# First transposes in another order, a longer run of dummy matmuls, and input forms ahead of other VectorE work, in a one-core attention and feed-forward kernel

## The chip, the cores and the metric

The kernel runs on one core of one Trainium2 chip. The metric is the device time of one execution in microseconds. In each pairing only executions on the same chip in the same rounds are compared. The span of a profile (first to last instruction) is about 1.8 us shorter than the device time of the same execution (723.8 against 725.55 us for the kernel before).

## The reference

Two branches on the same input `x` of 2048 rows by 1024 columns, in bfloat16, mixed by a gate:

```python
def reference(A_x, A_wqkv, A_wo, B_x, B_w_gate, B_w_up, B_w_down, gate_w):
    x = A_x
    g = _sigmoid((x * gate_w).sum(-1, keepdims=True))
    a = _A_ref(x, A_wqkv, A_wo)          # 32 heads of 32, 8 keys per query, 2 rows apart; then @ wo
    b = _B_ref(x, B_w_gate, B_w_up, B_w_down)   # (gelu(x@gate) * (x@up)) @ down, inner width 3584
    return g * a + (1 - g) * b
```

## The kernel before

The 2048 rows are four chunks of 512, worked on in two halves ("sup" 0 and 1, chunks 0-1 and 2-3). Most matrix products use seven block products in place of eight. For this VectorE computes sums and differences of blocks, called *forms*: of the weights, of the inputs (`x_forms`, in-place form T3 among them) and of the down projection.

A small scheduler orders everything. Each stream yields operations; at each step the operation with the smallest estimated start plus the stream's bias is emitted. The result is one fixed order per engine. An operation whose data have not come holds up those behind it: in the profile after, VectorE stands still for 0.9 us at one load with other work next in its order.

The head of the program: row loads, five dummy matmuls while they fly, and the load of the gate vector `gcol`, 1024 elements of 2 bytes.

```python
    for j in range(NST):
        (nc.sync if j % 2 == 0 else nc.scalar).dma_start(out=xrow(j, 0, KT), in_=x[j * P:(j + 1) * P, :])
    warm = hrow[:, XR + NST, 0:SC]
    nc.vector.memset(warm, 0.0)
    for i in range(5):
        nc.tensor.matmul(banks[7][:], lhsT=warm[:, 0:P], rhs=warm, start=True, stop=True)
    # ... (cut: exp table, identity, qsum)
    with nc.allow_non_contiguous_dma(reason="gate vector, one element per partition"):
        nc.gpsimd.dma_start(out=gcol[:], in_=gate_w.rearrange("(k p) -> p k", p=P))
```

The first work of TensorE: eight groups of four transposes, each group evicted by VectorE (even groups) or ScalarE (odd groups), then the q projection of chunk 0, whose first matmuls need the first half of the contraction of all four row tiles.

```python
    def main():
        ne = 0
        for j in range(NST):
            for k0 in range(0, KT, KH):
                # ... four transposes of tile j, half k0; eviction by VectorE if ne is even, else by ScalarE
        yield from qkv_outer(0)      # contraction slice by slice, as the weight slices land
        # ... (cut)
```

The input forms of a half, the last block of the weight preparation, and the transposing DMA of the attention, which shares SyncE's queue with the weight loads:

```python
    def x_forms():
        t = tt(KH * SC)
        for sup in range(NSUP):
            # ... t1, t2; then T3 in place, which waits for the gate matmul of the even chunk; then T4
            yield dve(t, lambda b12=b12, b22=b22: V(out=b12, in0=b22, in1=b12, op=ALU.subtract), [("z", c0)], key=("xf", sup, 3))

    def load_prep(i0):               # rows of w_down and of wo, for VectorE's down-projection weight forms
        # ...
                for k in range(n):
                    nc.sync.dma_start(out=st[:, 2 * h + k], in_=v[:, k])

        o = turn(n, taking("z", lambda: nc.sync.dma_start_transpose(out=rows("z"), in_=xbuf[:, accs[h], :])), [("qk", h)],
                 pre=xb_pre(), key=("acct", h))

    w.run([(0.0, main()), (0.0, loads()), (0.0, late_x()), (0.88, wforms()), (0.0, down_forms()), (0.1, x_forms()), (1.43, qkv_forms()),
           (1.3, preps()), (0.13, attention()), (0.36, scores())])
```

## Time and profile before

| | |
|---|---|
| device time | 725.25 us, median of 3 (725.22 to 725.55) |
| span of the profile | 723.8 us |
| TensorE busy | 713.6 us |
| first real matmul / start of the last one | 7.02 us / 719.70 us |
| 512-column matmuls after the head, from the order | 3280, at 0.216 us start to start: 708.5 us |

The head of the page of the kernel before, with busy time and its share of the span:

```profile
span 723.8 us, 9915 instructions
PE 713.6 (99%) x3314; PEld 351.1 (49%) x3381; DVE 598.5 (83%) x898; ACT 315.3 (44%) x535; POOL 71.8 (10%) x128
```

TensorE bounds the kernel; nothing but its waits, its head and its tail can be won without removing matmuls. The view of waits of the kernel before, TensorE only (who waited, for whom: us in total, times, longest):

```profile
PE ps L298 <- DVE hT L296: 1.2, 1, 1.2
PE ps L1252 <- DMA hT<-in_A_x_dram: 0.5, 1, 0.5
PE ps L628 <- DVE lend L481: 0.5, 1, 0.5
PE ps L995 <- ACT m L1049: 0.4, 1, 0.4
PE ps L496 <- DVE lend L1259: 0.3, 1, 0.3
```

The first, second and fifth lines are the head; the third is T3 at 321 us, the fourth the feed-forward stage at 176 us. "Idle" is counted from the modelled end of a matmul (0.379 us after its start at full speed), about 0.16 us after the next could have started (0.216 us start to start where nothing waits), so each real loss is a little larger. The head in the timeline (start, duration, engine, line):

```profile
0.86 0.27 DVE L296 MEMSET hT<- 128x256 uint32 x1 [0.86 <-PEq L1311]
1.19 2.32 PE L298 MATMUL ps<-hT 128*128 128x512 bf16 x5 [1.19 <-DVE hT L296]
1.34 1.04 POOL L310 DMA_DIRECT2D gcol<-in_gate_w_dram  x1 [0.33 <-issue]
...
4.04 2.69 PE L1252 MATMUL ps<-hT 128*128 128x128 bf16 x32 [0.53 <-DMA hT<-in_A_x_dram]
...
5.54 1.43 DVE L1259 COPY lend<-ps 128x512 bf16<-128x512 bf16 x3 [0.43 <-PE ps L1252]
5.87 1.56 ACT L1257 COPY lend<-ps 128x512 bf16<-128x512 bf16 x3 [0.18 <-PE ps L1252]
...
7.02 0.59 PE L496 MATMUL ps<-lend,hT 128*128 128x512 bf16 x2 [0.29 <-DVE lend L1259]
```

The transposes do not run at one speed. The windows view of their line shows how many are in flight or begun in each half microsecond (the count in brackets):

```profile
4.10:4.60 0.50, 0.50 (x6) 0.50 (x7) 1.00 1.03 397
4.60:5.10 0.50, 0.50 (x8) 0.50 (x6) 1.00 1.07 402
5.10:5.60 0.50, 0.50 (x7) 0.50 (x6) 1.00 1.73 350
5.70:6.20 0.50, 0.50 (x13) 0.50 (x11) 1.00 1.13 10
```

Single starts are 0.107 us apart up to 5.61 us and 0.056 us after: the clock steps up there. (Columns: window; its length; TensorE busy and count; weight loads busy and count; granted clock; DMA share; GB/s. The clock column is no help here: the trace's record of the granted clock begins at 5.61 us, at 1.00.)

The wait at 321 us in the chain of waits, before (start, us, what):

```profile
318.72 1.34 DVE ring L576 x4
320.06 1.15 DVE lend L481
321.21 0.05 issue
321.25 0.87 PE ps L628 x3
```

VectorE, without a pause, reaches T3 (L481) late, and TensorE (L628) starts as soon as it is done.

### The profile page before, as it was taken

The page shows a single profiled execution, that of the slowest core. Times are in us where ns is not written, and L with a number is a line of the kernel's source. Part 1 is how long each engine was busy: PE and PEld are TensorE (multiplying, and loading weights), DVE is VectorE, ACT ScalarE, POOL GpSimd, SP SyncE. Part 2 cuts the span into 40 slices and gives each one's busy share as a digit, 9 for nine tenths or more (in the row PEclk, how much of TensorE's full clock was granted, in tenths as well). Part 3 has the DMA queues.
Part 4 walks back from the last instruction along what each step waited for, and adds up shares of the span by engine and source line. Part 5 has one row for each costly group of instructions (what it writes and reads, how often), then busy time and mean ns, then how long its engine had stood idle before and what let it go on. Part 6 is the DMA issues. An engine that isn't in the chain of part 4 may idle for free.

```text
span 723.8 us, 9915 instructions
## 1 busy us (share of the span) xinstructions
PE 713.6 (99%) x3314; PEld 351.1 (49%) x3381; DVE 598.5 (83%) x898; ACT 315.3 (44%) x535; POOL 71.8 (10%) x128
## 2 busy tenths in 40 slices
PE   8999999999999999999999999999999999999997
PEld 5666644444444444455665444444444444444443
DVE  1799999999999899799599976999999995794200
ACT  2353465557655532035552114567558557110110
POOL 1000433343121100100000000000000000001000
PEclk9999999999999999999999999999999999999999
DMA  9944799989989979945239999786566657999992
GB/s 313 236 149 103 222 354 318 334 256 349 267 218 193 274 239 299 344 143 146 58 97 300 362 324 309 236 186 177 157 178 159 177 157 178 313 326 331 327 304 99
DMA packets 180931, 172.12 MB, mean 238 GB/s; under 512 B 56464, under 2 KB 137360, under 8 KB 180880
## 3 DMA queue, kind: packets, MB, share of 16 engines
q1 hardware_dynamic: 172048, 143.69, 68.5%
q0 software_dynamic: 8544, 27.27, 10.7%
q8 instruction: 26, 0.43, 0.2%
q10 hardware_dynamic: 288, 0.52, 0.2%
q14 instruction: 25, 0.20, 0.1%
HBM read 129.50 MB, written 28.31 MB: 218 GB/s over the span
## 4 chain that ended last, share of the span: by engine, by line
PE 83%; DVE 8%; DMA 4%; issue 4%; POOL 1%; ACT 0%; DVEq 0%; POOLq 0%; ACTq 0%
PE ps L995 35%; PE ps L1159 28%; PE ps L628 12%; PE ps L496 8%; DMA fforms<-ring 1%; DVE ring L457 1%; DVE ring L576 1%; DVE hT L1058 1%; DMA ring<-in_B_w_down_dram 1%; DMA ring<-in_A_wqkv_dram 1%; DMA hT<-in_A_wo_dram 1%; DMA hT<-in_B_w_down_dram 1%; DVE hT L1120 1%; DVE hT L1039 1%; DVE hT L433 0%
## 5 line engine op out<-in xcount | busy, mean ns | idle before, releaser
L995 PEld LDWEIGHTS <-ring 128*128 128x128 bf16 x1568 | 153.2, 98 | 185.8 <-issue 1.6
L995 PE MATMUL ps<-lend,ring 128*128 128x512 bf16 x877 | 210.5, 379 | 1.3 <-ACT m L1049 0.4
L995 PE MATMUL ps<-tf,ring 128*128 128x512 bf16 x659 | 162.6, 379 | 0.7
L1159 PE MATMUL ps<-ring,hT 128*128 128x512 bf16 x696 | 159.7, 379 | 0.6
L1159 PEld LDWEIGHTS <-hT 128*128 128x128 bf16 x708 | 69.2, 98 | 83.3
L945 DVE TENSOR_TENSOR xbuf<-xbuf,lend 128x2048 bf16<-128x2048 bf16 x64 | 77.4, 1215 | 7.5 <-DMA xbuf<-xbuf 7.5
L798 DVE TENSOR_TENSOR xbuf<-qo,lend 128x2048 bf16<-128x2048 bf16 x64 | 76.7, 1216 | 0.1
L804 DVE TENSOR_TENSOR xbuf<-xbuf 128x2048 bf16<-128x2048 bf16 x56 | 68.2, 1217 | 0.3
L628 PEld LDWEIGHTS <-ring 128*128 128x128 bf16 x384 | 49.3, 129 | 34.4 <-DVE lend L481 0.9
L1024 ACT COPY ps<-ps 128x512 f32<-128x512 f32 x56 | 32.0, 571 | 55.6 <-PE ps L995 55.5
L1067 ACT ACTIVATE gl<-ps 128x512 bf16<-128x512 f32 x56 | 33.5, 598 | 49.6 <-PE ps L995 48.5
L1194 ACT ACTIVATE ost<-ps,omg 128x512 bf16<-128x512 f32 x16 | 11.0, 688 | 100.6 <-PE ps L1159 81.9
L1186 POOL DMA_DIRECT2D out_dram<-ost x24 | 13.0, 540 | 411.0 <-ACT ost L1194 319.1
L1159 PE MATMUL ps<-ring,qo 128*128 128x512 bf16 x187 | 48.5, 379 | 0.2
L466 POOL DMA_DIRECT2D fforms<-ring x56 | 30.6, 546 | 175.3 <-DVE ring L457 166.1
L628 PE MATMUL ps<-lend,ring 128*128 128x512 bf16 x203 | 47.0, 380 | 0.7 <-DVE lend L481 0.5
L1039 DVE TENSOR_TENSOR hT<-hT,gl 128x1024 bf16<-128x1024 bf16 x56 | 38.3, 683 | 11.3 <-ACT hT L1036 11.3
L953 DVE TENSOR_TENSOR xbuf<-xbuf 128x1024 bf16<-128x1024 bf16 x64 | 42.0, 683 | 0.4
L1079 DVE TENSOR_TENSOR u<-ps,u 128x512 f32<-128x512 f32 x56 | 38.3, 684 | 4.6 <-PE ps L995 3.2
L628 PE MATMUL ps<-tf,ring 128*128 128x512 bf16 x173 | 40.1, 379 | 0.2
L1058 DVE TENSOR_TENSOR hT<-ps,m 128x512 bf16<-128x512 f32 x56 | 38.2, 683 | 1.5 <-PE ps L995 1.4
L1075 ACT COPY u<-ps 128x512 f32<-128x512 f32 x56 | 32.9, 587 | 15.1 <-PE ps L995 15.1
(110 smaller groups left out, 697.1 us busy)
## 6 DMA issues: line engine op xcount, KB each, us to landing
ring<-dforms SPq DMA_DIRECT2D x112, 256.0 KB, 5.3
ring<-in_B_w_down_dram SPq DMA_DIRECT2D x84, 256.0 KB, 4.6
ring<-in_B_w_gate_dram SPq DMA_DIRECT2D x56, 256.0 KB, 4.8
fforms<-ring POOLq DMA_DIRECT2D x56, 256.0 KB, 5.3
ring<-fforms SPq DMA_DIRECT2D x56, 256.0 KB, 4.0
ring<-in_B_w_up_dram SPq DMA_DIRECT2D x42, 256.0 KB, 4.7
ring<-in_A_wqkv_dram SPq DMA_DIRECT2D x32, 256.0 KB, 5.4
ring<-oforms SPq DMA_DIRECT2D x32, 256.0 KB, 5.7
```

The source lines that it names most:

```text
L496: nc.tensor.matmul(banks[bk][:], lhsT=lhsT, rhs=xT(c, kt), start=(kt == 0), stop=(kt == KT - 1))
L628: nc.tensor.matmul(banks[bk][:], lhsT=lhsT, rhs=rhs[:, kt, :], start=(start and kt == 0), stop=(kt == KH - 1), skip_group_check=True)
L798: V(out=w3(box[t]), in0=q_b, in1=k_w, op=ALU.mult)
L804: V(out=w3(box[0]), in0=w3(box[0]), in1=w3(box[t]), op=ALU.add)
L945: return dve(tt(n), taking(("p", t), lambda: V(out=w3(box["p", t]), in0=w3(box["ab"]), in1=v_w, op=ALU.mult)), [("qkv", c, 2, t), abo] + ( ...
L953: V(out=s4(t)[:, t % 2], in0=w3(box["p", t])[:, 0:4], in1=w3(box["p", t])[:, 4:8], op=ALU.add)
L995: nc.tensor.matmul(banks[bk][:], lhsT=wv[:, k, fl * P:(fl + 1) * P], rhs=rhs[:, k, :], start=(start and k == 0), stop=(k == KH - 1), skip_ ...
L1039: yield dve(tt(2 * SC), lambda f=f: nc.vector.tensor_tensor(out=hrow[:, f, :], in0=hrow[:, f, :], in1=gl[f][:], op=ALU.mult), [e, ev[f, "g ...
L1058: ev[f, "up2"] = dve(tt(SC, True), lambda f=f: nc.vector.tensor_tensor(out=hs(f, 1), in0=v3(banks[Bk[f]][:]), in1=v3(m5[f][:]), op=ALU.add ...
L1067: nc.scalar.activation(out=gl[f][:, SC:2 * SC], in_=banks[A[f]][:], func=ACT.Gelu_apprx_tanh)
L1079: e = dve(tt(SC, True), lambda f=f: nc.vector.tensor_tensor(out=u2[f][:], in0=banks[Dk[f]][:], in1=u2[f][:], op=ALU.add), [o, ev[f, "u2"]])
L1159: nc.tensor.matmul(banks[bk][:], lhsT=l, rhs=wv[:, i, :], start=(start and k == 0), stop=(q == last and i == 1), skip_group_check=True)
```

## The change

Its intent: have the first contraction half of all rows ready one group sooner; keep TensorE busy until the rows land so that its clock is up earlier than the 5.61 us of before; and let the input forms of a half go ahead of other VectorE work, so that TensorE does not wait for T3.

```diff
-    warm = hrow[:, XR + NST, 0:SC]
+    warm = xbuf[:, 0, 0:2]
     nc.vector.memset(warm, 0.0)
-    for i in range(5):
-        nc.tensor.matmul(banks[7][:], lhsT=warm[:, 0:P], rhs=warm, start=True, stop=True)
+    for n_ in [SC] * 6 + [P] * 3:
+        nc.tensor.matmul(banks[7][:, 0:n_], lhsT=warm[:, 0:1].to_broadcast([P, P]), rhs=warm[:, 1:2].to_broadcast([P, n_]),
+                         start=True, stop=True)
 ...
-        for j in range(NST):
-            for k0 in range(0, KT, KH):
+        for j, k0 in ((0, 0), (0, KH), (1, 0), (1, KH), (2, 0), (3, 0), (2, KH), (3, KH)):
+            if True:
 ...
-(0.1, x_forms())
+(-1.0, x_forms())
```

The bias acts on both halves: the input forms of chunks 0 and 1 move too. The order of TensorE's real work does not change.

More of the change, by code (lines that the diff above doesn't have):

```diff
@@ L1292, in main @@
                 yield from q_move(c0 + 3)
-    w.run([(0.0, main()), (0.0, loads()), (0.0, late_x()), (0.88, wforms()), (0.0, down_forms()), (0.1, x_forms()), (1.43, qkv_forms()),
+    w.run([(0.0, main()), (0.0, loads()), (0.0, late_x()), (0.88, wforms()), (0.0, down_forms()), (-1.0, x_forms()), (1.43, qkv_forms()),
            (1.3, preps()), (0.13, attention()), (0.36, scores())])
```

## The prediction

> **What bounds the kernel.** TensorE. The page's first part has PE busy 713.6 of 723.8 us, clock 0.999. By the program's order 3280 matmuls of 512 columns follow the dummies and first transposes; at the trace's 0.216 us start to start that is 708.5 of the 712.9 us between the first real matmul (7.02 us) and the end of the last (719.9). Gate matmuls explain about 2.5 us more. Left to win are the head and a few PE waits, in the view of waits and the single starts: 0.50 us at 321.25 (on T3, VectorE's in-place input form of the second half), 0.3 to 0.4 us at 176.15 (ScalarE's m copy, behind a 99% busy VectorE), about 0.15 us at 93.4. The 3.9 us tail is untouched.
>
> **What the change does.**
> 1. Dummies: 5 of 512 columns (427 ns apart from 1.19 us) become 6 of 512 and 3 of 128, after a smaller memset (0.27 us today). At the trace's cold pitches (427, 107 ns) they last 2.9 us, to about 3.9, so the 0.53 us gap before the transposes nearly closes. [...] the transposes' pitch drops from 107 to 56 ns at 5.61 us. [...]
> 2. Transposes: the first half of all rows is done after six groups, not seven, but PE still does all eight first. Today the first matmul waits 0.29 us for VectorE's fourth eviction (6.54 to 6.97); in the new order the last one needed is ScalarE's third, today 6.36 to 6.95. So with the clock as it is this gains 0 to 0.1 us. With an earlier clock, rows 2 and 3 land only at 5.29 and 5.51 us, and the second weight slice at 8.45, which suits a start at about 6.75. The head can hardly gain over 0.3 us.
> 3. Form order: PE's order is unchanged but for the dummies; VectorE's changes in about 140 lines. The first half's forms had slack. In the second half T3 (319.98 to 321.20) passes three down-projection forms (1.0 us each), two gate transposes (0.67) and four weight forms (0.34): about 5.8 us earlier, ending near 315.5; PE's 0.50 us wait goes. The last weight forms slide to about 322.9, just when PE reaches them: up to 0.2 us may come back.
> 4. Side effect: VectorE, 99% busy from 30 to 240 us, does weight forms, preparation and attention in another order. The waits at 93 and 176 us can vanish or grow by tenths.
>
> **Sum.** 725.25 - 0.1 (head) - 0.4 (T3 net) - 0.15 (others, either way) = **724.6 us**, range **723.8 to 725.4**. Faster by over 2%: 0.005; within 2%: 0.99; slower: 0.005.
>
> **What would show each step.** (1) PE's gap before the first transpose below 0.2 us; the clock step still near 5.6 us. (2) First real matmul at 6.75 to 7.05 us, waiting on ScalarE's copy or on weights. (3) No PE wait for T3 near 321 us; T3 ending near 315.5. (4) PE's other waits in the feed-forward part under 1 us in total.
>
> **What would make it wrong.** The clock stepping up well before the transposes, with weights landing sooner too; a VectorE order in which a form waits for a DMA and PE stalls by a microsecond or more between 90 and 240 us; a run-to-run move of the clock window as large as the effect.

The sum: 725.25 - 0.1 - 0.4 - 0.15 = 724.6 us. The "run-to-run move of the clock window" means that the step in the clock comes at another time in another execution.

## The result, and the profile after

Ratios are the mean time of one kernel's fast runs over that of the other's of the same rounds, so not quite the ratio of the medians.

| | before | after |
|---|---|---|
| device time, median of 4 | 725.24 us (724.96 to 725.55) | 725.35 us (724.95 to 725.68) |
| ratio | | 1.0001, 95% interval 0.9984 to 1.0018 |
| span of the profile | 723.8 us | 723.9 us |

The head of the page after, then TensorE's waits after:

```profile
span 723.9 us, 9988 instructions
PE 717.5 (99%) x3385; PEld 351.2 (49%) x3385; DVE 599.0 (83%) x898; ACT 315.2 (44%) x535; POOL 72.1 (10%) x128
```

```profile
PE ps L996 <- ACT m L1050: 1.0, 1, 1.0
PE ps L298 <- DVE xbuf L296: 0.9, 1, 0.9
PE ps L497 <- DMA hT<-in_A_wqkv_dram: 0.3, 1, 0.3
PE ps L497 <- ACT lend L1258: 0.2, 1, 0.2
PE ps L1253 <- DMA hT<-in_A_x_dram: 0.2, 1, 0.2
```

(The edit adds a line, so L995 before is L996 after.) The wait for T3 is gone. But a wait for a weight slice is new, and the wait in the feed-forward stage went from 0.4 to 1.0 us. The head in the timeline after:

```profile
0.81 0.06 DVE L296 MEMSET xbuf<- 128x1 uint32 x1 [0.81 <-PEq L1312]
0.93 3.06 PE L298 MATMUL ps<-xbuf 128*128 128x512 bf16 x9 [0.93 <-DVE xbuf L296]
...
4.04 1.16 PE L1253 MATMUL ps<-hT 128*128 128x128 bf16 x16
...
5.40 1.07 PE L1253 MATMUL ps<-hT 128*128 128x128 bf16 x16 [0.20 <-DMA hT<-in_A_x_dram]
5.84 0.87 DVE L1260 COPY lend<-ps 128x512 bf16<-128x512 bf16 x2 [0.40 <-PE ps L1253]
6.06 1.07 ACT L1258 COPY lend<-ps 128x512 bf16<-128x512 bf16 x2 [0.20 <-PE ps L1253]
...
6.70 0.81 PE L497 MATMUL ps<-lend,hT 128*128 128x512 bf16 x3 [0.23 <-ACT lend L1258]
...
8.87 0.65 PE L497 MATMUL ps<-lend,hT 128*128 128x512 bf16 x2 [0.28 <-DMA hT<-in_A_wqkv_dram]
```

Here the clock is up at 4.28 us, so all but the first three of the 32 transposes start about 0.056 us apart, not 0.107, where they do not wait; rows 2 and 3 land only at 5.36 and 5.55 us. The first real matmul comes at 6.70 us, 0.32 us sooner. At 8.87 us TensorE has used up the first weight slice and waits for the second.

At 313 to 321 us T3 (L482 now) ends at 316.4 us, and TensorE's product that needs it follows without a wait (timeline after):

```profile
315.20 1.22 DVE L482 TENSOR_TENSOR lend<-lend 128x2048 bf16<-128x2048 bf16 x1
...
319.71 3.62 PE L629 MATMUL ps<-lend,ring 128*128 128x512 bf16 x16
```

And the chain of waits after, up to the stall at 177 us:

```profile
160.77 1.60 SPq L356
...
164.24 8.95 DMA hT<-in_A_wo_dram
...
173.31 0.70 DVE hT L434
...
174.64 0.69 DVE u L1080
...
176.36 0.60 ACT m L1050
...
177.00 1.02 PE ps L996 x4
```

A load of `wo` rows, issued by SyncE at 164.24 us, lands at 173.18 us. VectorE has a weight form of it next in its order and stands still; behind that form stands the eviction (L1080) that ScalarE and then TensorE need. VectorE's waits from 150 to 180 us after (the same view of before has no line):

```profile
DVE hT L434 <- DMA hT<-in_A_wo_dram: 0.9, 1, 0.9
DVE ring L458 <- DMA ring<-in_B_w_gate_dram: 0.5, 1, 0.5
```

**The sum closes.** Since TensorE's order is the same, the two traces can be compared at fixed points of it: the first gate matmul of chunks 0, 1 and 2 (G0, G1, G2), the sum matmul after the q, k, v products of chunks 2 and 3 (S2), and the start of the last matmul.

| us | before | after | difference |
|---|---|---|---|
| G0 | 34.74 | 34.92 | +0.18 (first matmul -0.32, wait for the slice +0.50) |
| G0 to G1 | 52.83 | 52.83 | 0 |
| G1 to G2 (feed-forward, down) | 225.08 | 225.75 | +0.67 |
| G2 to S2 (contains T3) | 74.37 | 73.65 | -0.72 |
| S2 to last | 332.68 | 332.68 | 0 |
| last matmul starts | 719.70 | 719.83 | +0.13 |

### The profile page after: what moved, and what is told of

It reads as the page before. It is cut to its first block, busy times and chain, and to the rows that moved or that the text cites. A ratio compares the mean times of both kernels' runs of the same rounds, so it can differ in the third digit from the quotient of the medians.

```text
span 723.9 us, 9988 instructions
## 1 busy us (share of the span) xinstructions
PE 717.5 (99%) x3385; PEld 351.2 (49%) x3385; DVE 599.0 (83%) x898; ACT 315.2 (44%) x535; POOL 72.1 (10%) x128
## 4 chain that ended last, share of the span: by engine, by line
PE 96%; DMA 2%; SPq 1%; issue 0%; DVE 0%; ACT 0%; DVEq 0%
PE ps L996 45%; PE ps L1160 30%; PE ps L629 13%; PE ps L497 7%; DMA hT<-in_A_wo_dram 1%; DMA hT<-in_A_wqkv_dram 1%; SPq L356 0%; PE ps L736 0%; SPq L294 0%; DVE hT L434 0%; DVE u L1080 0%; ACT ost L1195 0%; ACT m L1050 0%; PE ps L760 0%; SPq L394 0%
## 5 line engine op out<-in xcount | busy, mean ns | idle before, releaser
L996 PEld LDWEIGHTS <-ring 128*128 128x128 bf16 x1568 | 153.2, 98 | 186.5 <-issue 2.3
L996 PE MATMUL ps<-lend,ring 128*128 128x512 bf16 x896 | 212.3, 379 | 1.1 <-ACT m L1050 1.0
L996 PE MATMUL ps<-tf,ring 128*128 128x512 bf16 x672 | 164.0, 379 | 0.0
L1080 DVE TENSOR_TENSOR u<-ps,u 128x512 f32<-128x512 f32 x56 | 38.4, 686 | 4.0 <-PE ps L996 2.9
```

The lines of the kernel that those rows point to most:

```text
L996: nc.tensor.matmul(banks[bk][:], lhsT=wv[:, k, fl * P:(fl + 1) * P], rhs=rhs[:, k, :], start=(start and k == 0), stop=(k == KH - 1), skip_ ...
L1080: e = dve(tt(SC, True), lambda f=f: nc.vector.tensor_tensor(out=u2[f][:], in0=banks[Dk[f]][:], in1=u2[f][:], op=ALU.add), [o, ev[f, "u2"]])
```

## The experiments

My theory A before the runs: three separate effects, all fixed by the orders. Rival B: the stall at 177 us is the chance of where a DMA lands. Rival C: the wait for T3 merely turns into one for later forms. All twelve runs gave the reference's result. Runs e1 to e4, e5 to e8 and e9 to e12 were three jobs, each with its own rounds of the kernel before (medians 725.60, 725.71 and 725.69 us).

What each profile showed, in us ("clock" is when full speed begins, the granted clock of 1.00 in the trace; "slice 2" when the second weight slice lands; a profile is one execution):

| | clock | slice 2 | G0 | G1 to G2 | G2 to S2 | time, median | ratio to before (95%) |
|---|---|---|---|---|---|---|---|
| before | 5.61 | 8.45 | 34.74 | 225.08 | 74.37 | 725.24 | |
| after | 4.28 | 8.82 | 34.92 | 225.75 | 73.65 | 725.35 | 1.0001 (0.9984 to 1.0018) |
| e1 | 6.60 | 8.56 | 35.25 | 225.43 | 73.66 | 726.30 | 1.0009 (0.9998 to 1.0021) |
| e2 | 9.22 | 8.66 | 36.26 | 225.86 | 73.65 | 725.50 | 1.0001 (0.9989 to 1.0013) |
| e3 | 8.02 | 8.74 | 35.64 | 225.44 | 73.76 | 726.58 | 1.0020 (1.0006 to 1.0034) |
| e4 | 3.64 | 8.87 | 34.97 | 225.09 | 73.76 | 725.19 | 0.9994 (0.9981 to 1.0007) |
| e5 | 4.14 | 7.38 | 34.56 | 225.07 | 73.75 | 724.89 | 0.9986 (0.9974 to 0.9998) |
| e6 | 5.94 | 7.22 | 34.91 | 225.07 | 73.65 | 725.02 | 0.9989 (0.9975 to 1.0002) |
| e7 | 3.82 | 6.96 | 34.42 | 225.07 | 73.65 | 724.81 | 0.9985 (0.9973 to 0.9997) |
| e8 | 4.42 | 8.65 | 34.93 | 226.68 | 73.65 | 727.52 | 1.0019 (1.0007 to 1.0032) |
| e9 | 4.85 | 9.38 | 35.48 | 225.08 | 75.08 | 725.71 | 0.9997 (0.9984 to 1.0011) |
| e10 | 5.46 | 9.35 | 35.45 | 225.08 | 73.76 | 725.62 | 0.9996 (0.9984 to 1.0009) |
| e11 | 9.31 | 8.69 | 36.21 | 225.08 | 73.76 | 726.34 | 1.0005 (0.9992 to 1.0017) |
| e12 | 3.76 | 6.97 | 34.37 | 225.69 | 73.65 | 725.28 | 0.9994 (0.9981 to 1.0006) |

S2 to last was 332.68 in all but e3 (333.08).

### e1: the changed kernel once more

No edit.

> The changed kernel once more, for what is order and what is chance. Theory A (three separate effects, fixed by the orders): first real matmul about 6.7 us, a wait of PE for the second weight slice near 8.9 us costing 0.3 to 0.6 us, PE start to start at 177 us about 1.4 us (1.2 us lost), no wait near 321 us; time within 0.3 us of before. Rival B (the loss at 177 us is the chance of where a load lands): that pitch can be anything from 0.4 to 1.4 us here, and below 0.8 us it would speak for B.

What I expected of T3 held (no wait near 321 us, G2 to S2 73.66). But the clock came at 6.60 us instead of 4.28, the first real matmul at 7.54 us, and no wait for the slice was left. The pitch (from the start of one matmul to the start of the next; 0.216 us where nothing waits) of the stall at 177 us was 1.11 us, between the 1.4 and the 0.75 of the two theories. The time was 0.70 us over the median of before, outside the 0.3 that I allowed. So the head is not fixed by the order; the clock moves from execution to execution.

### e2: early input forms in the second half alone

```diff
-    def x_forms():
+    def x_forms(sups):
...
-        for sup in range(NSUP):
+        for sup in sups:
...
-(0.1, x_forms())
+(0.1, x_forms([0])), (-1.0, x_forms([1]))
```

> Before, with the early input forms for chunks 2 and 3 alone; VectorE's order up to 300 us is that of before. Theory A: head as before (first matmul 7.02), pitch at 176 us about 0.75 us as before, no PE wait near 321 us, so 0.6 to 0.7 us faster than before: about 724.55. Rival B: the pitch at 176 us as likely to be 1.4 as 0.75. Rival C (the wait for T3 only turns into one for the last weight forms): PE still loses 0.3 us or more between 313 and 325 us, gain under 0.4 us.

Rival C falls: G2 to S2 is 73.65 us, the same to 0.01 us in all seven profiles with early second forms; nothing comes back. But theory A misses in two places. The time did not fall by 0.6 us; in the profiled execution the clock came at 9.22 us, and G0 1.5 us later than before. And the stall at 176 us grew to a pitch of 1.53 us with VectorE's *old* order, which is what rival B said could happen. VectorE's waits from 150 to 180 us in e2:

```profile
DVE hT L433 <- DMA hT<-in_A_wo_dram: 0.8, 1, 0.8
```

The last `wo` load was issued at 161.95 us and took 12.7 us to land; before it took 11.2 us and there was just no wait.

### e3: early input forms in the first half alone

```diff
-(0.1, x_forms())
+(-1.0, x_forms([0])), (0.1, x_forms([1]))
```

> Before, with the early input forms for chunks 0 and 1 alone. Theory A: this is the part that hurts: the first transposing DMA of the attention goes out near 60 instead of 56 us, the second near 155.7 instead of 153.3, the last Wo preparation load behind it near 160.8 instead of 158.4, VectorE waits about 0.9 us for it, PE pitch at 177 us about 1.4 us; the wait near 321 us is still there; 0.6 to 0.7 us slower than before, about 725.9. Rival B: pitch at 177 us near 0.75 us and the time of before.

Clear of noise and in the expected direction: 1.0020 (1.0006 to 1.0034). That is a ratio of means, and one execution of the six, 729.79 us, carries a third of it; the medians differ by 0.98 us, and without that execution the means by 0.89. The first transposing DMA of the attention went out at 60.8 us and the second at 156.5, VectorE waited 0.9 us for the `wo` load at 173.7 us; G1 to G2 grew by 0.36 us, less than the expected 0.6, because the load landed 8.8 us after its issue. A further 0.40 us came in after S2, at a wait near 554 us that no other run shows; the rest of this profile's loss is its head, with the late clock (G0 +0.90).

### e4: the head alone

```diff
-    warm = hrow[:, XR + NST, 0:SC]
+    warm = xbuf[:, 0, 0:2]
...  (dummies and transpose order as in the change; (0.1, x_forms()) kept)
```

> Before, with the new dummies and the new transpose order, the forms as before. Theory A: first matmul 6.7 us, but the second weight slice is waited for near 8.9 us and the first gate matmul (34.74 before) comes 0 to 0.2 us later or at most 0.2 earlier; the waits at 176 and 321 us as before; time within 0.2 us of before. If instead the head is worth its 0.3 us: gate at 34.4 us, and 0.3 us faster.

The clock was up at 3.64 us and the first matmul at 6.76 us, and yet G0 came 0.23 us *later* than before, slightly outside the 0.2 that I gave: the second slice landed at 8.87 us and TensorE lost about 0.7 us there. The wait at 176 us was as before. The wait for T3 was not: G2 to S2 was 73.76, with VectorE's order unchanged. So the 0.72 us that early forms won between the two first profiles is mostly luck of the profile of before; typical is 0.11 us.

### e5: the head, with the gate vector's DMA late

The same kernel, with the DMA of 2-byte elements moved from the start to a point after the second k eviction:

```diff
-    with nc.allow_non_contiguous_dma(reason="gate vector, one element per partition"):
-        nc.gpsimd.dma_start(out=gcol[:], in_=gate_w.rearrange("(k p) -> p k", p=P))
...
+    def gate_vector():
+        def fn():
+            with nc.allow_non_contiguous_dma(reason="gate vector, one element per partition"):
+                nc.gpsimd.dma_start(out=gcol[:], in_=gate_w.rearrange("(k p) -> p k", p=P))
+        yield Op("POOL", (0, 1.0), fn, [("qkv", 0, 1, 1)], after=True)
...
-    w.run([(0.0, main()),
+    w.run([(0.0, main()), (0.0, gate_vector()),
```

> Head part alone (as e4), and the gate vector's DMA (1024 elements of 2 bytes, landing near 8 us, beside the weight slices) issued only after the second k evacuation, about 25 us. Theory: this DMA is what makes the second weight slice land 2.3 us after the first. Then that slice lands before 7.8 us and PE has no wait for weights; the gate matmul 0.3 to 0.7 us earlier than in e4 for a clock step at the same time (34.3 to 34.5 us with a step before 4.5 us, near 34.9 with a step at 6.6). Rival (the weights are late of themselves, from the row loads): slice still at 8.4 us or later, and the wait stays when the clock is early.

The second slice landed at 7.38 us, and TensorE had no wait for weights. Here is DMA traffic from 5 to 9 us in 40 slices before (busy tenths, then GB/s), with the queues:

```profile
DMA  9998999988900002442145989999999999999999
GB/s 369 369 471 348 389 172 65 44 1 1 4 0 0 0 21 82 143 82 82 41 184 225 328 307 369 410 410 430 389 410 369 430 389 410 389 430 410 389 389 451
...
q1 hardware_dynamic: 552, 1.02, 67.5%
q0 software_dynamic: 32, 0.00, 30.0%
```

and in e5:

```profile
DMA  9999999999999999999999999999999799998999
GB/s 389 410 389 369 389 349 410 389 410 389 410 389 369 410 410 430 389 389 369 451 389 389 369 410 410 348 328 410 410 389 348 287 246 328 348 348 348 430 451 348
...
q1 hardware_dynamic: 829, 1.52, 101.8%
```

Before, the rate is under 190 GB/s for 1.6 us (5.5 to 7.1 us), and at most 4 GB/s for 0.6 us of it, while queue 0, which carries the gate vector, holds 30% of the engines' time with almost no bytes. In the packet records of the trace its data are 16 packets of 128 bytes (64 elements each) that take 0.89 to 1.39 us apiece; from 6.1 to 6.4 us all 16 are under way together and take nearly the whole time of the 16 DMA engines. In e5 the mean from 5 to 9 us is 381 GB/s, with no such stretch. G0 came at 34.56 us (0.06 outside my range: now the *first* slice, landing at 6.74 us, held the first matmul until 6.79). The time is 0.9986 of before, an interval clear of 1. In the four kernels with the vector late the second slice landed at 6.96 to 7.38 us; in the ten with it early, at 8.45 to 9.38.

### e6: e5 and early forms in the second half alone

> e5 plus the early forms of the second half alone (e2). The order up to 300 us on VectorE is that of before. From the traces so far: pair stage of chunks 2 and 3 (gate matmul to sum matmul) 73.65 us as in every kernel with early second forms, against 73.76 to 74.37 without. Pitch at 176 us: 0.75 if the last Wo load lands within about 85 us of the gate matmul of chunk 1, up to 1.5 otherwise. Time: 0.3 to 1.0 us faster than before in the mean of the rounds.

All as expected: 225.07 and 73.65 us, the last `wo` load 83.6 us after G1, no VectorE wait there; time 0.69 us under the median of before, though with the clock at 5.94 us G0 was no better than before in this execution.

### e7: e6, the last four wo loads on GpSimd's queue

```diff
-                    nc.sync.dma_start(out=st[:, 2 * h + k], in_=v[:, k])
+                    (nc.gpsimd if i0 == NPREP - 2 else nc.sync).dma_start(out=st[:, 2 * h + k], in_=v[:, k])
```

> e6 with only the last four Wo preparation loads moved from SyncE's queue (where they stand behind the second transposing DMA) to GpSimd's. No other instruction moves. Theory: they are issued 1 to 5 us earlier, land before VectorE needs them, no VectorE wait there; pitch at 176 us at most 0.76. Rival: the landing is set by the traffic of that stretch, not by the queue: they land as late as ever, or the stores that now follow them on GpSimd do harm.

The loads landed 81.1 us after G1, against 83.6 in e6 and 85.5 in e2; the pitch at 176 us was 0.74. That is the floor with this order: about 0.5 us is lost there with VectorE never waiting, just late. The lowest median of all kernels, 724.81 us.

### e8: the changed kernel, with the same four loads on GpSimd's queue

The edit of e7 on the changed kernel.

> The changed kernel with the same four loads moved to GpSimd's queue. Theory: VectorE's wait of 0.7 to 0.9 us at 173 us goes, the pitch at 177 us falls from 1.1-1.4 to about 0.75; 0.35 to 0.65 us faster than e1 for the same clock step. Rival (traffic): wait and pitch as in e1.

A miss. The wait for the `wo` load went, as the theory said, and a longer one took its place. VectorE's waits from 150 to 180 us in e8:

```profile
DVE ring L458 <- DMA ring<-in_B_w_gate_dram: 2.3, 1, 2.3
```

The gate block's loads stand behind the second transposing DMA in SyncE's queue too. In the kernels with early first-half forms that DMA goes out 67.98 to 67.99 us after G1 in all five (after, e1, e3, e8, e12), in the other nine 65.74 to 65.78 us after. Gate block and `wo` rows then come in one late batch, and whichever of them lands last is waited for. Pitch at 178 us 1.91 us; 1.0019 of before (1.0007 to 1.0032), slower clear of noise.

### e9: the dummies alone

> Before with the new dummies alone. Theory: it is the dummies that move the clock step (seen so far at 3.6 to 6.6 us with the long run, at 5.6, 8.0 and 9.2 us with the short one), not the transposes. Expected: step between 3.5 and 6.9 us; with a step before 4.6 us the first real matmul at 6.65 to 6.85, so within 0.1 us of the new transpose order, and then a wait for the second weight slice; time within 0.3 us of e4, 0 to 0.7 us faster than before in the mean. Rival: the transpose order is what brings the first matmul forward, so here it stays near 7.0 even with an early clock.

The clock came at 4.85 us, as expected of the dummies. The first matmul came at 7.24 us, not 6.7, but on neither theory's account: the first weight slice landed at 7.19 us. The evictions had been done: the last one needed in the old transpose order ended at 6.67 us. So the inputs were ready early without the new order, which speaks for the theory, though the first matmul itself could not show it. The time was a miss: 725.71 us, 0.02 above the median of before and 0.52 above e4's (of another job). G2 to S2 is the worst of all, 75.08: VectorE waited for a DMA of the attention near 300 us and reached T3 later still. VectorE's waits from 290 to 325 us in e9, and TensorE's for T3:

```profile
DVE xbuf L946 <- DMA xbuf<-xbuf: 1.6, 1, 1.6
```

```profile
PE ps L629 <- DVE lend L482: 1.2, 1, 1.2
```

In before the same DMA wait was 0.9 us, and it had none over 0.3 us in e3, e4, e5, e10 and e11 (the other kernels with late second forms), where T3 cost 0.10 to 0.11 us. With early second forms waits of 0.3 to 0.6 us for that DMA (after, e1, e6, e12) cost nothing.

### e10: the transpose order alone

> Before with the new transpose order alone. Theory: worth nothing, since TensorE still does all 32 transposes first and the third ScalarE eviction ends as late as VectorE's fourth did: first matmul 0.40 to 0.50 us after the start of the last transpose, as in all kernels so far; step at 5.5 us or later; time within 0.3 us of before. Rival: 0.2 us or more from last transpose to first matmul is saved, below 0.3 us.

From the start of the last transpose to the first matmul 0.49 us, as expected (the clock came at 5.46 us, a hair before the 5.5 that I gave). In e10 ScalarE's third eviction ended at 6.86 us and VectorE's fourth at 6.88: with the old order TensorE would have waited for the second of these. The order is worth 0.02 us here and 0.06 in e12 (6.61 and 6.67). It may be worth more with a late clock: in e2, e3 and e11, old order, where the clock came after the last transpose, ScalarE's third eviction ended 0.27 us before VectorE's fourth (7.59 and 7.86 us in e2). That 0.27 us is an estimate from those traces; no run has the new order with so late a clock.

### e11: no dummies

```diff
-    for i in range(5):
-        nc.tensor.matmul(banks[7][:], lhsT=warm[:, 0:P], rhs=warm, start=True, stop=True)
```

> Before with no dummy matmuls at all, to measure what the clock is worth. Theory [...]: the step comes between 6.5 and 10.2 us, transposes all cold (last one starts near 7.4), first matmul near 7.9, gate matmul between 35.4 and 36.8 us; 0.3 to 1.0 us slower than before in the mean, with as wide a spread. Rival: the dummies do nothing: time as before.

The clock came at 9.31 us, after all the transposes; first matmul 7.73 us, G0 36.21 us. In the medians 0.65 us slower than before, but the interval (0.9992 to 1.0017) contains 1.

### e12: the whole change, with the gate vector late

The edit of e5 on the changed kernel.

> The changed kernel with the gate vector's DMA late: the head of e5, the forms of the change. Theory: head as e5; first-half forms still cost: second transposing DMA of the attention near 68 us after the gate matmul of chunk 1 (65.75 with the old order), VectorE waits for a gate weight block near 166 us and/or a Wo load near 173 us, the stage from there to the gate matmul of chunk 2 225.4 us or more (225.07 with the old order); time 0.3 us or more above e5 and e6, near 725.3. Rival: with the head put right the change is worth its whole gain, time 724.9 or below.

As expected: head 34.37 us, the best of all; the second transposing DMA 67.99 us after G1; VectorE waits of 0.5 and 0.9 us; G1 to G2 225.69. 725.28 us, 0.39 us above e5 (which ran in another job, so this difference is weaker than the ratios). Putting the head right does not free the change of the cost of its first-half forms.

## Why the prediction was right or wrong

The time, 725.35 us, lies in the range, near its upper end, and "within 2%" was right. The expected gain of 0.6 us did not come. That the time is inside the range says little: the range held "no change" as well, by 0.15 us, and effects of +0.85 and -0.72 us that I had not foreseen at that size happened to cancel. The first rounds alone would not even exclude the gain (0.9991 lies in 0.9984 to 1.0018); those of e1 do (0.9998 to 1.0021).

**Bound.** Right: TensorE's stages agree to 0.01 us between kernels wherever it does not wait (S2 to last 332.68 us in 13 of the 14 profiles). One reading was wrong: the "0.15 us at 93.4" was no wait. The start to start there, 0.525 us, is, as I read it, one missing record of 0.216 us and the 0.309 us that before shows at its other changes to a small matmul (at 34.43, 59.30, 87.26, 312.34 and 386.71 us); in after, the same start to start, at 93.28 us, is 0.309. That stage did not change.

**Step 1, dummies.** The gap closed as said (0.05 us); the first real matmul, at 6.70 us, was just ahead of the 6.75 to 7.05 that I gave, which is luck: the same kernel had it at 7.54 us in e1. "The clock step still near 5.6 us" is what failed. With the long dummies the clock came at 3.64 to 6.60 us in nine profiles, with the short ones at 5.46 to 9.22 in four, with none at 9.31. In each of the 14 profiles the stretch that the trace records at a granted clock of 1.00 is 716.80 us (as in before) or 720.21 us (as in after) long. The two differ by 3.41 us, and are 210 and 211 times 3.413.

So I counted TensorE's work in stretches of 3.413 us back from the step, each matmul as busy for its start-to-start time (0.427 us for 512 columns and 0.107 us for 128 before the step). The last stretch before the step has a share of 0.78 (before) to 0.94 in the 14 profiles, and earlier ones have 0.74 (e3) at most. The transposes are part of that: without them the last stretch in before would have 0.32, and a stretch of 0.73 in e2 was followed by no step. With the modelled ends of the records the two sets touch (0.79 and more, 0.80 and less), so a limit is not shown, nor that the share is the cause; shown is that the clock came earlier with the longer dummies (at 4.61 us in the mean of the nine, 7.08 in that of the four), and after the fuller stretches. As an estimate from the two traces: the 3.41 us up to 4.28 us had 0.90 in after, and the short dummies of before would have filled 0.70 of them. What remains is a difference between executions with the same head: the step came at 5.61 us in before and 9.22 in e2, at 4.28 in after and 6.60 in e1. With it G0 moves by over a microsecond (34.74 us in before, 36.26 in e2), which I had named as a thing that would make the prediction wrong. What part of the spread of the times it makes is not measured, since one execution of each run was traced.

**Step 2, transposes.** Right that the order gains 0 to 0.1 us (0.02 and 0.06 in e10 and e12), and that an earlier clock is capped by the second weight slice (with the clock at 4.28 us in after, the slice landed at 8.82 and TensorE waited until 8.87). The term that was mis-sized: I took the slice to land at 8.45 us as in the one profile; it landed at 8.56 to 9.38 in the nine others with the gate vector early, so the early start turned into a wait and G0 got 0.18 us *later*, not 0.1 us earlier. e5 shows the cause: without the gate vector's DMA in the head the slice landed at 7.38 us. In before, those 2 KB (1024 elements of 2 bytes, 16 packets of 128 bytes) went with a fall of the rate from about 390 GB/s to under 190 for 1.6 us, and to almost nothing for 0.6 us of it. With it early the slice on the other queue landed about 1.7 us later in the mean of the profiles (8.45 to 9.38 us in ten, 6.96 to 7.38 in the four with it late).

**Step 3, T3.** The mechanism was right: T3 ended at 316.4 us (I said near 315.5), its wait went, and nothing came back of the 0.2 us that I feared. The size was off both ways: 0.72 us in this pair of profiles where I had -0.4 net, and 0.11 us in five of seven kernels with late second forms. The other two (before 0.72, e9 1.43) had VectorE held by a DMA near 300 us (for 0.9 and 1.6 us). Early forms are an insurance against that DMA more than a steady gain.

**Step 4, the other order of VectorE.** I gave the waits at 176 us a few tenths either way and all of TensorE's waits there under 1 us (the view shows 1.0, by start to start 1.2 us were lost), and for the first half I wrote that its forms "had slack". They had; what they displaced had none. What I had named as a thing that would make the prediction wrong, a form that waits for a DMA while TensorE stalls by a microsecond or more between 90 and 240 us, is what happened, at 173 to 177 us. The scores of chunk 0 finish later (the first transposing DMA, of its first half, leaves 25.2 us after G0 in place of 21.2), the second transposing DMA leaves 2.2 us later relative to TensorE, and weight loads are queued behind it (the `wo` loads are issued from 160.77 us on, in before from 158.37). G1 to G2 was 225.43 to 226.68 us in all five kernels with early first-half forms, and 225.07 to 225.09 in eight of the other nine (225.86 in e2). So theory A and rival B each had a part: the order takes the slack away, the landing decides how much is lost, and even the old order loses it once in nine.

**What stays open.** The rounds put the first-half forms at about 1 us (e3 against before, in the medians), the profiles at 0.36 to 0.67 us in this stage (1.60 in e8, where the loads were also moved); whether other executions stall more, or the clock's step fell late, profiles of single executions cannot say. The gain of T3 in e2's rounds is inside the noise. I have not shown what made the slices land later in some runs than in others.

A version that beats the kernel before came out of it (it was not run in the same rounds as the changed one): e7 (long dummies, new transposes, late gate vector, early forms in the second half alone, four loads on GpSimd), 724.81 us, 0.9985 of before (0.9973 to 0.9997). That is 0.15%, well inside "the same" at 2%. Against e6, which lacks only the moved loads, and e5, which has the old forms too, it is not separated.

## What to carry to other kernels

In a kernel whose bounding engine is 99% busy, add up its waits first: that sum, here 1.7 us of 725 in the view of waits after the dummies start, is most of the prize (what its work loses at the lower clock comes on top: about 0.8 us here, an estimate from 15 transposes of before at 0.107 in place of 0.056 us), and compare traces at fixed points of that engine's order, where differences close to a hundredth of a microsecond. When an early stage is made faster, look up what it will wait for next, and on what else the arrival of that thing depends; and when an operation is moved forward, ask what the displaced operations release, above all a DMA with other loads behind it in the same engine's queue (here the second transposing DMA, out 2.2 us later). One profile is one draw: in the 14 here the clock's step fell anywhere from 3.64 to 9.31 us and G0 from 34.37 to 36.26 (together with the slices' landing and the dummies), while the wait for T3 varied by 1.3 us. A wait that depends on a landing or on the clock's step needs several profiles before it is called a property of the kernel.
